# Reordering the casts, splits and sums of one expert's second layer in a kernel whose order is written out by hand

## The chip, the cores and the metric

The kernel runs on one core of a Trainium2 chip. The metric is the device time of one execution in microseconds (us), the median of several runs. Beside the times there is a profile of one execution, taken by the hardware profiler. Its engines are PE (TensorE matmul), PEld (TensorE weight load, which overlaps PE), DVE (VectorE), ACT (ScalarE), POOL (GpSimd) and SP (SyncE, which only issues DMAs here). Every engine takes its instructions strictly in the order in which the kernel emits them, and waits at one whose inputs are not ready, whatever stands behind it.

## The reference

```python
def reference(q, k, v, domain_probs, w1, w2):
    x = pooled_attention(q, k, v) + local_attention(q, k, v)   # [2, 8, 576, 64] each
    x = x.transpose(0, 2, 1, 3).reshape(1152, 512)
    p = domain_probs / (domain_probs.sum(-1, keepdims=True) + 1e-09)
    out = 0
    for e in range(4):                                         # four experts, every token
        h = np.maximum(x @ w1[e], 0.0)                         # 512 -> 1024
        out += p[:, e:e + 1] * (h @ w2[e])                     # 1024 -> 512
    return out                                                 # [1152, 512] float32
```

## The kernel before

The kernel computes the attention first, then the four experts, which the code numbers e = 0 to 3; the second expert is e = 1. Each layer of an expert is computed on 2x2 blocks with seven block products in place of eight, in the manner of Strassen: sums and differences of blocks of the tokens (or of H, the hidden rows) are multiplied with sums and differences of weight blocks. The products of a layer are called "1" to "7"; the second layer takes them in the order 1, 5, 2, 6, 7, 4, 3, so the first is "1" and the fourth is "6". To keep float32 accuracy each operand is split in two float32r tiles: a high part (a cast) and a low part (the operand minus its high part). A product is three passes of matmuls: low x high, high x low, high x high.

Each product of the second layer is done in two halves of 256 tokens. All work is cut into named steps, and one list, ORDER, gives the order in which steps are emitted; a step goes to the instruction queue of its engine. The steps around the change, with e = 1 as the first digit after the letters (for s, c and dt as shown):

- `s110`, `s111`, `s510`, `s511`, `s210`, `s211`, `s610`, `s611`, `s710`: on PE (L1239), 24 matmuls each: the two halves of the products 1, 5, 2, 6 and 7. `c11` and `c21` (L1252, 24 matmuls each) do the 128 tokens in the middle.
- `ah120.0`, `ah121.0`, `ah160.0`, `ah161.0`: on ACT (L1146, L1150), the high part of H for product 2 (halves 0 and 1) and product 6, 128x1024 each. They write a "unit" tile; there are three such tiles in a ring, so each cast waits for the matmuls that read the same tile three halves earlier: `ah120.0` waits for `s111`, `ah121.0` for `s510`, `ah160.0` for `s511`, `ah161.0` for `s210`.
- `ao120.0`, `ao121.0`, `ao160.0`, `ao161.0`: on DVE (L1155, L1159), the low parts of the same. `s210` needs `ao120.0`, `s211` needs `ao121.0`, `s610` needs `ao160.0`, `s611` needs `ao161.0`.
- `as16.0`, `as16.1`, `as17.0`: on DVE (L1133), the sums of H blocks for the products 6 and 7. `ah160.0` needs both `as16` steps.
- `bl12.0`, `bl13.0` (SP, L1093) and `bl17.1` (POOL, L1095, an adding DMA): load the raw second-layer weights of products 2, 3 and 7 into one raw buffer, so `bl13.0` waits for `bo12` and `bl17.1` for `bo13`.
- `bh12`, `bh13`, `bh17` (ACT, a cast at L186) and `bo12`, `bo13`, `bo17` (DVE, L1101): the high and low parts of these weights. `s210` needs `bo12`; `s710` needs `bo17`; `bo13` is needed only after `s710`.
- `dt1x10`, `dt1x11`, `dt1y0` (ACT, L1297, two instructions each): copy a finished PSUM bank, scaled, into a part tile; `dd1x10`, `dd1x11` (POOL, L1300) add the part tile to the accumulator by DMA. There is one part tile, so `dt1x11` waits until `dd1x10` has landed, and `dt1y0` until `dd1x11` has. `s610` needs `dt1x10`, `s611` needs `dt1x11`.
- `th1` (ACT, L1210) and `to1` (DVE, L1212): the middle tokens' high and low parts, which `c11` needs; `tdh1` (ACT, L1218) and `tdo1` (DVE, L1220) the same for `c21`.

The rules that tie a cast to its ring tile and to its inputs, in the code's own words:

```python
                    deps = deps + users[RING[n % 3]]
                    step(f"ah{e}{m}{h}.{g}", "A", deps, lambda m=m, h=h, fs=fs: high(m, h, fs))
                    step(f"ao{e}{m}{h}.{g}", "V", [f"ah{e}{m}{h}.{g}"], lambda m=m, h=h, fs=fs: low(m, h, fs))
                users[RING[n % 3]] = [f"s{m}{e}{h}"]
```

and the loop that emits the program:

```python
    for name in order(steps):
        steps[name][2]()
```

Of the kernel before, what the change touches and what calls it, by code (L numbers as in the profile page):

```python
# [68 lines left out]
    p612 wo13 p512 t1212 h2111 wm204 p712 wl20 t2212 as15.0 p113 p212 t1113 bh15 p613 h1112 wa2042 bo15 p513 t1213  # L69
    dd0y1 ao110.0 h2212 p713 t2213 p312 h2213 ah110.1 p412 h1212 ao110.1 ah111.1 ao111.0 ao111.1 s110 ah150.0 h2112  # L70
    p413 bl12.0 h2113 ao150.0 bh16 bo16 p213 wm206 p313 wm205 wa2052 bl14.1 h1113 as15.1 h1213 ah150.1 s111 ah151.0
    wa2023 ao150.1 ah151.1 ao151.0 dt1x10 ao151.1 th1 as16.0 dd1x10 bh12 bo12 bl13.0 s510 ah120.0 as16.1 bh13 ao120.0
    s511 ah121.0 bo13 ao121.0 bl17.1 s210 ah160.0 wa2020 ao160.0 dt1x11 as17.0 s211 ah161.0 dd1x11 ao161.0 s610
    ah170.0 to1 ao170.0 tr1 s611 ts1 ah171.0 d1x20.0 wa2062 d1x20.1 bh17 ao171.0 c11 dt1y0 bo17 bh14 dd1y0 d1x21.0
    bl21.0 ah140.0 d1x21.1 as13.0 s710 tdh1 tdo1 ao140.0 s711 ah141.0 d1x30.1 wh20 d1x30.0 ao141.0 c21 ah130.0 bo14
    dt1y1 d1x31.1 bl26.0 d1x31.0 dd1y1 wo20 s410 ao130.0 wl21 s411 d1z10.0 ah131.0 d1z10.1 d1z11.0 d1z11.1 ao131.0
# [1338 lines left out]
```

## Time and profile before

| what | value |
|---|---|
| time, median of 3 runs | 441.28 us (441.1 to 443.62) |
| profiled execution, its own time | 439.78 us |
| span of the profiled execution | 438.1 us |
| PE busy | 430.1 us (98% of the span) |
| DVE busy | 337.7 us (77%) |
| ACT busy | 224.2 us (51%) |
| POOL busy | 107.8 us (25%) |
| DMA | 46.72 MB, mean 107 GB/s |

The span runs from the first to the last recorded instruction; the profiled execution's own time is 1.68 us longer than its span. Busy shares are averages over stages with different limits, so they only say which engine to look at first; what a change in one place is worth has to be read from the instructions in that place.

### The profile page before, as it was taken

How to read it: one execution, taken by the hardware profiler on the slowest of the kernel's cores; microseconds unless marked ns; L12 is line 12 of the kernel's file. 1: busy time of each engine (PE TensorE's matmuls, PEld its weight loads, DVE VectorE, ACT ScalarE, POOL GpSimd, SP SyncE). 2: the span in 40 equal slices, each digit the busy share in tenths (PEclk: the TensorE clock that was granted, in tenths of full speed). 3: DMA queues.
4: the chain of work that ended last, by engine and by line, in shares of the span. 5: the costliest groups of instructions: out<-in, count | busy, mean ns of one | idle time of the engine just before them, and what ended most of it. 6: DMA issues, size and time to landing. Idle time of an engine off the chain costs nothing.

```text
span 438.1 us, 10188 instructions
## 1 busy us (share of the span) xinstructions
PE 430.1 (98%) x4221; PEld 412.7 (94%) x4221; DVE 337.7 (77%) x560; ACT 224.2 (51%) x430; POOL 107.8 (25%) x133
## 2 busy tenths in 40 slices
PE   8999999999999999999989999999999999999997
PEld 8757998998999999999989999999999999999996
DVE  2778989989899988464989874669899736688983
ACT  3547576435567634444456253555564355446540
POOL 4148781423212120021331211023312110013010
PEclk9999999999999999999999999999999999999999
DMA  9889934337708464343764854066746731145135
GB/s 170 154 242 178 171 80 94 61 87 170 143 0 121 113 146 104 49 102 79 120 97 86 177 112 74 1 156 114 104 84 137 131 76 22 49 96 79 20 97 168
DMA packets 81784, 46.72 MB, mean 107 GB/s; under 512 B 37194, under 2 KB 80714, under 8 KB 81738
## 3 DMA queue, kind: packets, MB, share of 16 engines
q1 hardware_dynamic: 63674, 29.95, 27.4%
q0 software_dynamic: 18064, 16.12, 25.8%
q8 instruction: 33, 0.54, 0.5%
q14 instruction: 13, 0.11, 0.1%
HBM read 39.63 MB, written 2.36 MB: 96 GB/s over the span
## 4 chain that ended last, share of the span: by engine, by line
PE 93%; DVE 3%; ACT 2%; DMA 1%; issue 1%; POOL 0%; ACTq 0%; POOLq 0%
PE ps L1239 34%; PE ps L1046 30%; PE ps L1252 5%; PE m02h L833 5%; PE m01h L833 4%; PE m00h L833 3%; PE wps L275 2%; PE vs L480 1%; DVE slot L1101 1%; DMA raw<-in_moe_w_dram 1%; PE a_qt L404 1%; ACT slot L186 1%; PE a_qt L402 1%; PE k01t L402 1%; PE k00t L402 1%; PE a1pv L646 1%
## 5 line engine op out<-in xcount | busy, mean ns | idle before, releaser
L1239 PE MATMUL ps<-slot,unit 128*128 128x256 f32 x1344 | 161.6, 281 | 2.4 <-DVE unit L1155 2.4
L1239 PEld LDWEIGHTS ps<-slot,unit 128*128 128x128 f32 x1344 | 160.0, 189 | 2.9 <-DVE unit L1155 2.8
L1046 PE MATMUL ps<-xhi,slot 128*128 128x288 f32 x384 | 66.5, 295 | 0.0
L1095 POOL DMA_DIRECT2D raw<-in_moe_w_dram x20 | 27.0, 1350 | 146.1 <-DVE slot L1101 112.5
L1046 PE MATMUL ps<-xc,slot 128*128 128x288 f32 x432 | 60.2, 295 | 0.0
L1046 PEld LDWEIGHTS ps<-xc,slot 128*128 128x128 f32 x432 | 58.2, 188 | 0.0
L1046 PEld LDWEIGHTS ps<-xhi,slot 128*128 128x128 f32 x384 | 56.2, 188 | 0.0
L186 ACT CAST slot<-raw 128x1024 fp32r<-128x1024 f32 (+1 forms) x40 | 49.1, 1237 | 13.0 <-DVE raw L994 4.8
L1058 ACT ACTIVATE H<-ps 128x288 f32<-128x288 f32 x72 | 27.9, 412 | 50.5 <-PE ps L1046 49.2
L1062 DVE TENSOR_TENSOR H<-H,ps 128x288 f32<-128x288 f32 x72 | 29.7, 449 | 19.6 <-PE ps L1046 19.6
L1146 ACT ACTIVATE unit<-H 128x512 fp32r<-128x512 f32 (+1 forms) x32 | 26.4, 844 | 32.2 <-DVE H L1062 18.7
L1101 DVE TENSOR_TENSOR slot<-raw,slot 128x1024 fp32r<-128x1024 f32 x28 | 34.1, 1225 | 9.9 <-ACT slot L186 9.9
L1000 DVE TENSOR_TENSOR slot<-raw,slot 128x1792 fp32r<-128x1792 f32 x12 | 24.3, 2021 | 22.2 <-PE ps L1046 18.6
L1046 PE MATMUL ps<-xlo,slot 128*128 128x288 f32 x192 | 41.1, 295 | 0.0
L1150 ACT ACTIVATE unit<-H 128x1024 fp32r<-128x1024 f32 x24 | 25.2, 1059 | 30.4 <-PE ps L1239 15.7
L1133 DVE SCALAR_TENSOR_TENSOR H<-H 128x1024 f32<-128x1024 f32 (+1 forms) x24 | 37.6, 1575 | 0.8 <-ACT H L1060 0.5
L1159 DVE SCALAR_TENSOR_TENSOR unit<-H,unit 128x1024 fp32r<-128x1024 f32 x24 | 29.3, 1220 | 7.4 <-ACT unit L1150 7.4
L988 POOL DMA_DIRECT2D raw<-in_moe_w_dram x12 | 18.4, 1594 | 52.1 <-DMA raw<-in_moe_w_dram 52.1
L1155 DVE SCALAR_TENSOR_TENSOR unit<-H,unit 128x512 fp32r<-128x512 f32 (+1 forms) x32 | 29.8, 952 | 1.4 <-ACT unit L1146 1.3
L1046 PEld LDWEIGHTS ps<-xlo,slot 128*128 128x128 f32 x192 | 30.8, 188 | 0.0
L1265 DVE SCALAR_TENSOR_TENSOR acc<-ps,npr,acc 128x256 f32<-128x256 f32 x56 | 24.3, 476 | 4.7 <-PE ps L1239 4.7
L1252 PE MATMUL ps<-slot,slot 128*128 128x256 f32 x192 | 24.3, 282 | 0.0
(290 smaller groups left out, 591.4 us busy)
## 6 DMA issues: line engine op xcount, KB each, us to landing
raw<-in_moe_w_dram POOLq DMA_DIRECT2D x20, 512.0 KB, 6.2
raw<-in_moe_w_dram SPq DMA_DIRECT2D x16, 512.0 KB, 4.0
raw<-in_moe_w_dram SPq DMA_DIRECT2D x24, 256.0 KB, 3.9
vw<-in_v_dram SPq DMA_DIRECT2D x44, 64.0 KB, 3.5
acc<-in_q_dram SPq DMA_DIRECT2D x12, 192.0 KB, 4.3
acc<-in_k_dram SPq DMA_DIRECT2D x12, 192.0 KB, 4.8
out_dram<-acc SPq DMA_DIRECT2D x18, 128.0 KB, 1.8
raw<-in_moe_w_dram SPq DMA_DIRECT2D x2, 1024.0 KB, 6.6
```

The costliest lines, as they stand in the source:

```text
L186: nc.scalar.copy(out_, in_)
L833: nc.tensor.matmul(ps[:, :n], w[:, d, cc:cc + P], x[:, d, n0:n0 + n], start=i == 0 and d == 0, stop=i == 2 and d == HP - 1,)
L1046: nc.tensor.matmul(bank(acc_, n, i)[:, :NH // 2], w[:, d * P:(d + 1) * P], x[:, d, n * (NH // 2):(n + 1) * (NH // 2)], start=u == 0 and fi ...
L1058: nc.scalar.mul(dst, at, -1.0)
L1062: nc.vector.tensor_tensor(dst, dst, at, ALU.add)
L1095: nc.gpsimd.dma_start(raw2(q), src, accum_op=ALU.add)
L1101: engine(f"bo{e}{m}").tensor_tensor(w2tile(m, 1), raw2(q), f32(w2tile(m, 0)), ALU.subtract)
L1133: nc.vector.scalar_tensor_tensor(at[o], at[x], 0.0, at[y], ALU.max, op)
L1155: nc.vector.scalar_tensor_tensor(o, x, 0.0, y, ALU.max, ALU.subtract)
L1159: nc.vector.scalar_tensor_tensor(o, x, -1.0, y, ALU.mult, ALU.subtract)
L1239: nc.tensor.matmul(ps[:, t * 256:t * 256 + 256], a[:, f, t * P:t * P + P], b[:, f], start=first_ and (t, f, x) == (0, 0, 0), stop=(t, f, x ...
L1252: nc.tensor.matmul(w, a[:, 2 * f + r], b[:, f], start=(c, r, f, x) == (1, 1, 0, 0), stop=(r, f, x) == (0, 3, 2), skip_group_check=True,)
```

## The change

Two lines of ORDER are changed, and nothing else. They cover the stretch from the last casts of product 5 to the fourth product of expert 1.

```diff
-    wa2023 ao150.1 ah151.1 ao151.0 dt1x10 ao151.1 th1 as16.0 dd1x10 bh12 bo12 bl13.0 s510 ah120.0 as16.1 bh13 ao120.0
-    s511 ah121.0 bo13 ao121.0 bl17.1 s210 ah160.0 wa2020 ao160.0 dt1x11 as17.0 s211 ah161.0 dd1x11 ao161.0 s610
+    wa2023 ao150.1 ah151.1 ao151.0 bh12 ao151.1 bo12 bl13.0 ah120.0 dt1x10 ao120.0 th1 as16.0 dd1x10 s510 ah121.0
+    as16.1 ao121.0 s511 ah160.0 ao160.0 bh13 bo13 bl17.1 s210 wa2020 dt1x11 as17.0 s211 ah161.0 dd1x11 ao161.0 s610
```

Sorted by engine, this is what changes. The orders on PE, POOL and SP stay the same.

```
ACT before: ah151.0 ah151.1 dt1x10 th1 bh12 ah120.0 bh13 ah121.0 ah160.0 dt1x11 ah161.0
ACT after:  ah151.0 ah151.1 bh12 ah120.0 dt1x10 th1 ah121.0 ah160.0 bh13 dt1x11 ah161.0
DVE before: ao151.0 ao151.1 as16.0 bo12 as16.1 ao120.0 bo13 ao121.0 ao160.0 as17.0 ao161.0
DVE after:  ao151.0 ao151.1 bo12 ao120.0 as16.0 as16.1 ao121.0 ao160.0 bo13 as17.0 ao161.0
```

## Rows read from the trace of the kernel before

**Rows 1.** Groups of instructions by line: busy us, mean ns, idle before and releaser.
```profile
L1239 PE MATMUL ps<-slot,unit 128*128 128x256 f32 x1344 | 161.6, 281 | 2.4 <-DVE unit L1155 2.4
L1239 PEld LDWEIGHTS ps<-slot,unit 128*128 128x128 f32 x1344 | 160.0, 189 | 2.9 <-DVE unit L1155 2.8
```
**Rows 2.** Timeline of PE: start, us, instructions, idle before and releaser.
```profile
209.30 8.71 PE L1239 MATMUL ps<-slot,unit 128*128 128x256 f32 x72
218.87 3.13 PE L1239 MATMUL ps<-slot,unit 128*128 128x256 f32 x24 [0.86 <-DVE unit L1155]
223.56 8.77 PE L1239 MATMUL ps<-slot,unit 128*128 128x256 f32 x72 [1.56 <-DVE unit L1155]
232.16 3.04 PE L1252 MATMUL ps<-slot,slot 128*128 128x256 f32 x24
235.04 5.86 PE L1239 MATMUL ps<-slot,unit 128*128 128x256 f32 x48
240.73 3.04 PE L1252 MATMUL ps<-slot,slot 128*128 128x256 f32 x24
```
**Rows 3.** Chain of work that ended last, from 200 us: start, us, what.
```profile
216.57 3.47 DMA raw<-in_moe_w_dram
...
221.14 1.23 DVE slot L1101
222.37 1.15 DVE unit L1155
```
**Rows 4.** Timeline of DVE.
```profile
211.65 1.90 DVE L1157 TENSOR_TENSOR unit<-H,unit 128x512 fp32r<-128x512 f32 x3
...
215.31 1.23 DVE L1101 TENSOR_TENSOR slot<-raw,slot 128x1024 fp32r<-128x1024 f32 x1 [0.63 <-ACT slot L186]
216.46 1.22 DVE L1133 SCALAR_TENSOR_TENSOR H<-H 128x1024 f32<-128x1024 f32 x1
217.59 1.22 DVE L1155 SCALAR_TENSOR_TENSOR unit<-H,unit 128x1024 fp32r<-128x1024 f32 x1
...
224.56 2.28 DVE L1133 SCALAR_TENSOR_TENSOR H<-H 128x2048 f32<-128x2048 f32 x1
...
232.69 1.22 DVE L1101 TENSOR_TENSOR slot<-raw,slot 128x1024 fp32r<-128x1024 f32 x1
...
236.81 0.68 DVE L1220 TENSOR_TENSOR slot<-H,slot 128x512 fp32r<-128x512 f32 x1
```
**Rows 5.** Timeline of ACT.
```profile
212.56 0.84 ACT L1297 ACTIVATE part1x<-ps,pr 128x256 f32<-128x256 f32 x2
213.28 1.06 ACT L1210 ACTIVATE slot<-H 128x1024 fp32r<-128x1024 f32 x1
214.24 1.05 ACT L186 CAST slot<-raw 128x1024 fp32r<-128x1024 f32 x1
215.17 1.07 ACT L1146 ACTIVATE unit<-H 128x1024 fp32r<-128x1024 f32 x1
220.06 1.05 ACT L186 CAST slot<-raw 128x1024 fp32r<-128x1024 f32 x1 [3.83 <-DMA raw<-in_moe_w_dram]
...
231.57 0.83 ACT L1297 ACTIVATE part1y<-ps,pr 128x256 f32<-128x256 f32 x2
```
**Rows 6.** Timeline of POOL.
```profile
213.69 1.20 POOL L1300 DMA_DIRECT2D acc<-part1x  x1 [1.95 <-ACT part1x L1297]
222.67 1.28 POOL L1095 DMA_DIRECT2D raw<-in_moe_w_dram  x1 [7.78 <-DVE slot L1101]
...
224.13 2.30 POOL L1300 DMA_DIRECT2D acc<-part1x  x1
```
**Rows 7.** SP's weight loads at L1093, 190 to 245 us: instructions, then time to landing.
```profile
L1093 SPq DMA_DIRECT2D raw<-in_moe_w_dram x4: 368/368/368, 195.6 to 241.8; - x4
...
DMA to landing us min/median/max: 3.5/4.2/4.9
```
**Rows 8.** POOL's adding weight loads at L1095, 205 to 250 us: time to landing.
```profile
DMA to landing us min/median/max: 5.8/5.8/6.9
```
**Rows 9.** POOL's adding DMAs of the part tiles at L1300, whole span: time to landing.
```profile
DMA to landing us min/median/max: 3.7/4.3/6.4
```

## The prediction

> **What bounds the kernel now.** I read the page first: PE is busy nearly all the span, so an edit that moves no matmul can only pay where PE stands still. The second view is the groups by line. The second layer's matmuls (L1239) stood still for 2.4 us in the whole execution, all of it for DVE's low parts at L1155 [rows 1]. The third view, PE's timeline, puts this idle time in one place, the second layer of expert 1: 0.86 us ahead of `s210` at 218.87 and 1.56 us ahead of `s211` at 223.56 [rows 2]. So the change works on the only stretch of the second layers where PE waits, and its ceiling is the price of these two gaps.
>
> The chain that ended last says where the second gap comes from. `bo12` lets `bl13.0` go, which lands 3.47 us later; ACT had been standing at `bh13` for 3.83 us; then `bo13`, and only behind it `ao121.0`, for which PE waits [rows 3, 5]. But `s211` doesn't need `bh13` or `bo13` at all: their weights are for product 3, the last of the seven. They are only queued ahead of what it needs. The first gap has the same form with less in front: `ao120.0` ran at 217.59 to 218.81, behind `as16.0`, `bo12` and `as16.1` [rows 4], and `s210` does not need the sums.
>
> **What the gaps are worth.** From `s211` to `c11` three halves took 232.16 - 223.56 = 8.60 us, so an undisturbed half takes 2.87 us from start to start. `s111`, `s510` and `s511` ran from 209.30 in one piece, so `s210` could start at 209.30 + 8.60 = 217.90 and `s211` at 220.77. It started at 223.56: the two gaps delay all that follows by 2.79 us [rows 2]. The two idle figures add up to 0.86 + 1.56 = 2.42 us, less, since a matmul's end overlaps the next one's start. The ends of matmuls in this trace are modelled and the starts recorded; I take 2.79 and keep 2.42 as the low end.
>
> The weight loads of the same line stood still for 2.8 us for the same releaser [rows 1]. [...]
>
> **The change, step by step.** Nothing is added or removed; I lay the same instructions in the new order, with start-to-start distances of the old one. On ACT these are 0.72 for a drain pair, 0.96 for a cast after `th1` and 0.93 between casts (I take 0.96 for each cast) [rows 5]; on DVE 1.15 after a weight split and 1.13 after a sum [rows 4].
>
> ACT is free for the first moved step at 212.56 [rows 5]. `bh12` now takes that place; `bl12.0`, the first of the four loads, left at 195.6 and even the slowest took 4.9 us [rows 7], so its data are there. `bh12` runs 212.56 to 213.61, `ah120.0` 213.52 to 214.59 (`s111`, whose tile it takes, ended about 212.2), `dt1x10` from 214.48, `th1` from 215.20, `ah121.0` 216.16 to 217.23 (`s510` ended about 215.0).
>
> DVE ends the low parts of product 5 at 213.55 and meets `bh12`'s end at 213.61 [rows 4], so the new wait in front of `bo12` costs it under 0.1 us. Then `bo12` 213.63 to 214.86, `ao120.0` 214.78 to 216.00, `as16.0` from 215.91, `as16.1` 217.04 to 218.26, `ao121.0` 218.17 to 219.39. PE wants `ao120.0` at 217.90 and `ao121.0` at 220.77: spare time 1.9 and 1.4 us, where both were late. **Both gaps close: -2.79 us.**
>
> What is late next? I follow each queue past the end of the change.
>
> `ah160.0` needs `as16.1` (218.26) and `s511` (about 218.0): 218.3 to 219.36; `ao160.0` ends about 220.6, wanted by `s610` at 223.63. Spare 3.0.
>
> `bh13` is now queued behind it. `bl13.0` leaves when `bo12` ends, about 214.9 in place of 216.57, and lands 3.5 to 4.9 us later, 218.4 to 219.8 [rows 3, 7]; ACT gets there at 219.3. So the 3.83 us stall of ACT becomes at most 0.5. `bo13` 220.5 to 221.7 (at most 222.1), then `as17.0` from 221.66, 2.90 us earlier than its 224.56 [rows 4], and `ao161.0` 223.9 to 225.1, wanted by `s611` at 226.50. Spare 1.4 (1.0 with the slow landing). DVE was full behind `as17.0` and moves by as much as PE does.
>
> `dt1x10` and so `dd1x10` come later: in the old order the DMA left at 213.69, 0.29 after the drain's end [rows 5, 6]; now at 215.6. With 3.7 to 6.4 us to landing [rows 9] it lands at 219.3 to 222.0, and `dt1x11` stands for it on ACT, which gets there at 220.2. This is a **new wait of 0 to 1.8 us**, with `ah161.0` queued behind. `ah161.0` then ends by 223.8, and DVE wants it at 223.9: covered, barely in the slow case, and PE only at 226.50.
>
> `bl17.1` follows `bo13` and so moves by only 0.6 us. It leaves 0.3 us after it, at 222.0, and lands 5.8 to 6.9 us later [rows 3, 6, 8]: 227.8 to 228.9. `bh17` needs 1.05 more, 230.0 at the latest; `bo17`, at 232.69 before [rows 4], has its turn at 232.69 - 2.90 = 229.8 and ends by 231.3. `s710` wants it at 235.04 - 2.79 = 232.25. Spare 0.95 to 1.2; it was 1.1.
>
> `dd1x11` stands 1.46 us behind `bl17.1` on POOL [rows 6], so it leaves at 223.5 and with the longest landing, 6.4 [rows 9], is there at 229.9. `dt1y0` waits for it and would stand on ACT at 231.57 - 2.79 = 228.8 [rows 5]: a second new wait of up to 1.1 us. Behind it comes what `tdo1` and `c21` need; `tdo1` ended at 237.49, 3.2 us ahead of `c21` [rows 2, 4]. Covered.
>
> **The sum.** -2.79 us, nothing given back. The profiled execution would go from 439.78 to 437.0, its span from 438.1 to 435.3. Its time lay 1.5 below the median of the runs, 441.28, so I subtract from the median: 438.5 us, 0.6% faster. About 1% is what a measurement of this kernel can tell from no change, so the step counts as "within 1%" although I expect it to be real.
>
> **Rivals.** (a) *The gap is moved on, in part.* The tightest spare times left are about 1 us (`ao161.0`, `bo17`). For it: two ACT waits that the old order didn't have, and `bl17.1` moving less than PE. Against: all landings of the trace fit. A landing 1 us beyond the longest, or some tenths at each of five steps, would leave 0.5 to 1.5 us of the gain lost: about 439.5.
>
> (b) *Slower: ACT held at `dt1x11` by the part tile.* `dd1x10` now leaves after `bl13.0`, not 2.9 us before it. `s611` is hurt only if `ah161.0` ends after 225.2, that is if `dd1x10` lands after 223.4, 7.8 us from its issue; each further us is then 1 us on PE. It eats the whole gain at 10.6 us; at 13 us, twice the longest in the trace, the kernel is 2.4 us slower, 443.7. Against: no landing of this line is above 6.4 [rows 9]. [...]
>
> (c) *The change doesn't do what it says*: another wait, hidden behind those shown (a shared semaphore, a dependency of the sums of H on the casts that read the same tile), keeps `ao121.0` near 222. Then 441 to 441.5. The rows speak against it: `ao120.0` and `ao121.0` start within 0.1 us of the end of the DVE work ahead of them [rows 3, 4], so queueing held them, not data.
>
> **How the numbers follow.** Full recovery 0.80 (438.5; 438.9 with the low end of the price), (a) 0.11, (b) 0.04, (c) 0.05. The range: below, the full 2.79 and about 1.0 for the scatter of a median (the three runs lay between 441.1 and 443.62), 437.5; above, (a) at its far end, 440.0, with the same scatter, 441.0. Faster by over 1% would take 4.4 us, more than all the idle time in reach: 0.04 for scatter alone. Slower by over 1% needs (b) at its far end or a scattered median: 0.04. Within 1%: 0.92.
>
> **What would show it.** Right: in the changed kernel's timeline of PE seven halves (168 matmuls) from `s111` to `s611` stand in one piece, some 20.1 us long, and the groups by line show near 0 idle at L1239; ACT no longer stands at `bh13`; `bo13` runs behind `ao160.0`; PE's last matmuls come 2.8 us earlier. `dt1x11` may show a wait for a DMA. Wrong: a gap at `s611` or `s710`, whose releaser names rival (a) or (b); a gap still at `s211` means (c); no gap and the same time would mean that the idle time was given back in the experts behind.

## The result and the profile after

The changed kernel takes 436.51 us in the median of 9 runs (436.07 to 439.43), the kernel before 441.1 us beside it (439.61 to 443.62): a ratio of 0.9907, 95% interval 0.988 to 0.9935. (A ratio and its interval, here and below, come from the single runs, without any that lies over 1.5% above the fastest of its kernel; the quotient of the two medians is 0.9896.) It is faster, as forecast, but by 3 to 5 us where 2.8 was said, and 436.5 lies below the range that was given, 437.5 to 441. The profiled execution went from 439.78 to 436.1 us.

The groups by line in the changed kernel: the second layer's matmuls wait for nothing any more, where there were 2.4 us [rows 1].

```profile
L1239 PE MATMUL ps<-slot,unit 128*128 128x256 f32 x1344 | 160.9, 280 | 0.0
L1239 PEld LDWEIGHTS ps<-slot,unit 128*128 128x128 f32 x1344 | 159.8, 189 | 0.1
```

PE's timeline of the changed kernel (start, us, instructions): the seven halves from `s111` to `s611` stand in one piece.

```profile
208.54 20.09 PE L1239 MATMUL ps<-slot,unit 128*128 128x256 f32 x168
228.47 3.04 PE L1252 MATMUL ps<-slot,slot 128*128 128x256 f32 x24
231.35 5.86 PE L1239 MATMUL ps<-slot,unit 128*128 128x256 f32 x48
```

From `s111` to `c11` it takes 228.47 - 208.54 = 19.93 us, where it took 232.16 - 209.30 = 22.86 [rows 2]: 2.93 us, near the 2.79 of the forecast. The spans differ by 438.1 - 434.4 = 3.7. The other 0.76 is there before the change begins: `s111` itself starts 0.76 us earlier, after instructions that are the same in both kernels.

ACT's timeline of the changed kernel, from `bh12` on (add 0.76 to a time to compare it with the rows of before):

```profile
211.80 1.05 ACT L186 CAST slot<-raw 128x1024 fp32r<-128x1024 f32 x1
212.75 1.05 ACT L1146 ACTIVATE unit<-H 128x1024 fp32r<-128x1024 f32 x1
213.72 0.82 ACT L1297 ACTIVATE part1x<-ps,pr 128x256 f32<-128x256 f32 x2
...
215.38 1.05 ACT L1146 ACTIVATE unit<-H 128x1024 fp32r<-128x1024 f32 x1
217.63 1.06 ACT L1150 ACTIVATE unit<-H 128x1024 fp32r<-128x1024 f32 x1 [1.20 <-DVE H L1133]
218.59 1.03 ACT L186 CAST slot<-raw 128x1024 fp32r<-128x1024 f32 x1
219.53 0.83 ACT L1297 ACTIVATE part1x<-ps,pr 128x256 f32<-128x256 f32 x2
...
229.42 0.84 ACT L1297 ACTIVATE part1y<-ps,pr 128x256 f32<-128x256 f32 x2 [1.12 <-DMA acc<-part1x]
```

And DVE's:

```profile
212.88 1.23 DVE L1101 TENSOR_TENSOR slot<-raw,slot 128x1024 fp32r<-128x1024 f32 x1
214.02 1.22 DVE L1155 SCALAR_TENSOR_TENSOR unit<-H,unit 128x1024 fp32r<-128x1024 f32 x1
215.16 2.35 DVE L1133 SCALAR_TENSOR_TENSOR H<-H 128x1024 f32<-128x1024 f32 x2
217.43 1.22 DVE L1155 SCALAR_TENSOR_TENSOR unit<-H,unit 128x1024 fp32r<-128x1024 f32 x1
218.72 1.23 DVE L1159 SCALAR_TENSOR_TENSOR unit<-H,unit 128x1024 fp32r<-128x1024 f32 x1
219.86 1.22 DVE L1101 TENSOR_TENSOR slot<-raw,slot 128x1024 fp32r<-128x1024 f32 x1
...
229.12 1.22 DVE L1101 TENSOR_TENSOR slot<-raw,slot 128x1024 fp32r<-128x1024 f32 x1
```

`ao120.0` ends at 215.24 and `ao121.0` at 218.65; PE comes to `s210` at 208.54 + 8.6 = 217.1 and to `s211` at 220.0, so both are early by 1.9 and 1.4 us, as worked out. `bh13` (218.59) no longer stands for its load. `dt1x11` (219.53) shows no wait for `dd1x10`, and `dt1y0` (229.42) shows the second new wait, 1.12 us, hidden. Everything behind `c11` only moves: from its start to the end of the span it takes 438.1 - 232.16 = 205.9 us before and 434.4 - 228.47 = 205.9 after.

So the mechanism was there and the gain in one profile had the right size. What was open was the difference between the times, over 4 us against 2.9.

### The profile page after: what moved, and what is told of

The parts are those of the page before. It is cut to its first block, busy times and chain, and to the rows that moved or that the text cites. A ratio compares the mean times of both kernels' runs of the same rounds, so it can differ in the third digit from the quotient of the medians.

```text
span 434.4 us, 10187 instructions
## 1 busy us (share of the span) xinstructions
PE 429.2 (99%) x4221; PEld 412.2 (95%) x4221; DVE 337.8 (78%) x560; ACT 224.2 (52%) x430; POOL 107.8 (25%) x133
## 4 chain that ended last, share of the span: by engine, by line
PE 97%; DVE 1%; ACT 1%; issue 0%; POOL 0%; POOLq 0%; ACTq 0%
PE ps L1239 36%; PE ps L1046 31%; PE ps L1252 5%; PE m02h L833 5%; PE m01h L833 4%; PE m00h L833 3%; PE wps L275 2%; PE vs L480 1%; PE a_qt L404 1%; PE a_qt L402 1%; PE k01t L402 1%; PE k00t L402 1%; PE a1pv L646 1%; PE a3pv L646 1%; PE a3sl L562 0%; PE a2sl L562 0%
## 5 line engine op out<-in xcount | busy, mean ns | idle before, releaser
L1095 POOL DMA_DIRECT2D raw<-in_moe_w_dram x20 | 27.0, 1351 | 142.8 <-DVE slot L1101 108.1
```

Source lines behind the costliest of these rows:

```text
L1095: nc.gpsimd.dma_start(raw2(q), src, accum_op=ALU.add)
```

## The experiments

The theory at the start: the change is worth the gap, 2.9 us, and the rest is chance ahead of it. Its first rival: the new order itself shortens what stands ahead of it. The first four runs also take the two halves of the change apart. Kernels that were timed together share the runs of the kernel before.

**e1 and e2: both kernels again, unchanged.**

> The kernel before, unchanged, timed once more as a kernel of its own. It measures what two identical kernels differ by, and gives a second profile of the stretch before the change. Theory P (the change is worth 2.9 us, read from s111's start to c11's start: 22.86 us before, 19.93 us after; the rest of the 4.6 us between the medians is scatter of the stretch before the change, which is the same code in both): no difference from before within 0.3%, s111 to c11 at 22.8 to 22.9 us again, and the start of s111 anywhere within about 1 us of 209.3. Rival S (the new order makes the stretch ahead of it shorter too, by 0.76 us in the profile): s111 starts near 209.3 again in every kernel that has the old order, and near 208.5 in every one that has the new.

> The changed kernel, unchanged, timed once more beside the kernel before. Theory P: s111 to c11 at 19.9 us again; start of s111 scattered as in the kernel before; ratio near 0.9934 (2.9 us of 441). Rival S: start of s111 near 208.5, ratio near 0.9907 again (4.1 us).

e1: ratio 1.0012 (0.9988 to 1.0036), as it must be. e2: 436.89 us, 0.9907 (0.9873 to 0.994), as in the first series. 2.9 us, a ratio of 0.9934, lies at the edge of either interval, so one series alone would not have refuted the theory; the same 4 us twice speak against it. PE's timeline in the profile of e1, and the load in its chain of waits:

```profile
209.67 8.70 PE L1239 MATMUL ps<-slot,unit 128*128 128x256 f32 x72
219.24 3.12 PE L1239 MATMUL ps<-slot,unit 128*128 128x256 f32 x24 [0.86 <-DVE unit L1155]
224.45 8.77 PE L1239 MATMUL ps<-slot,unit 128*128 128x256 f32 x72 [2.10 <-DVE unit L1155]
```
```profile
216.94 4.00 DMA raw<-in_moe_w_dram
```

In the same kernel the second gap is 2.10 us this time, not 1.56, because `bl13.0` landed after 4.00 us and not after 3.47 [rows 3]; the first gap, which waits for no DMA, is 0.86 again. In e2 `s111` to `c11` took 19.93 us again, and `s111` began at 209.21, 0.67 later than in the first profile of the same kernel: what stands ahead of the change scatters by itself. So each side missed one of its signs: the theory the ratio, the rival the early start of `s111`.

**e3: the first half of the change alone.**

```diff
-ACT: dt1x10 th1 bh12 ah120.0 bh13 ah121.0 ah160.0    DVE: as16.0 bo12 as16.1 ao120.0 bo13 ao121.0 ao160.0
+ACT: bh12 ah120.0 dt1x10 th1 bh13 ah121.0 ah160.0    DVE: bo12 ao120.0 as16.0 as16.1 bo13 ao121.0 ao160.0
```

> Only the weights and operand of product 2's first half go forward (bh12, ah120.0 ahead of dt1x10 and th1; bo12, ao120.0 ahead of as16.0); bh13 and bo13 stay ahead of ah121.0 and ao121.0. Theory P: the gap ahead of s210 closes (0.97 us). bl13.0 leaves 1.7 us earlier too, so bh13 begins at about 218.4 to 219.8 on the time axis of before, bo13 ends at 220.7 to 222.1 and ao121.0 at 221.8 to 223.2, for which s211 waits from 220.8: a gap of 1.0 to 2.4 us is left, 0.4 to 1.9 us gained, s111 to c11 21.0 to 22.4 us. If the waits were not those of the queue (rival: a hidden dependency of ao121.0), the second gap would keep its end at 223.56 and the gain would be 0.

**e4: the second half alone.**

```diff
-ACT: dt1x10 th1 bh12 ah120.0 bh13 ah121.0 ah160.0    DVE: as16.0 bo12 as16.1 ao120.0 bo13 ao121.0 ao160.0
+ACT: dt1x10 th1 bh12 ah120.0 ah121.0 ah160.0 bh13    DVE: as16.0 bo12 as16.1 ao120.0 ao121.0 ao160.0 bo13
```

> Only bh13 and bo13 go back, behind ah160.0 and ao160.0; the start of the stretch keeps the old order (dt1x10, th1, bh12, ah120.0; as16.0, bo12, as16.1, ao120.0). Theory P: s210 waits as before, until 218.87 (0.97 us lost), and s211 no longer, since ao121.0 ends at about 220.0 and s211 is due at 221.7: 1.8 to 1.9 us gained, s111 to c11 about 21.0 us. If the second gap were set by something other than the order of bo13 and ao121.0, 0 to 0.5 us gained.

PE's timeline in e3, then in e4:

```profile
211.85 11.58 PE L1239 MATMUL ps<-slot,unit 128*128 128x256 f32 x96
224.98 8.77 PE L1239 MATMUL ps<-slot,unit 128*128 128x256 f32 x72 [1.55 <-DVE unit L1155]
233.58 1.60 PE L1252 MATMUL ps<-slot,slot 128*128 128x256 f32 x12
```
```profile
208.65 8.71 PE L1239 MATMUL ps<-slot,unit 128*128 128x256 f32 x72
218.22 11.65 PE L1239 MATMUL ps<-slot,unit 128*128 128x256 f32 x96 [0.86 <-DVE unit L1155]
229.70 3.04 PE L1252 MATMUL ps<-slot,slot 128*128 128x256 f32 x24
```

`s111` to `c11`: 21.73 us in e3 (its load took 4.01 us) and 21.05 in e4, both as expected; each half closes its own gap. The times: e3 440.02 us, ratio 0.9976 (0.995 to 1.0002, so its 1.1 us are not clear of no change); e4 438.09 us, 0.9934 (0.9909 to 0.9959), 2.9 us faster than before where 1.8 to 1.9 were expected. By the traces e3 should lie 21.73 - 19.93 = 1.8 us above the changed kernel (436.89 in e2, timed beside it) and lies 3.1 above. The kernels whose PE waits for `bl13.0`'s landing are slower than their profiles say; e4, whose PE does not, isn't (1.1 by the trace, 1.2 measured).

**e5: the old order, with the load early.** To let the load go early, `bh12` and `bo12` move forward with it, which takes `bo12` out of the first gap; `bh13` and `bo13` stay where they were. This separates the landing from the queues.

```diff
-... bl12.0 h2113 ao150.0 bh16 bo16 p213 wm206 p313 wm205 wa2052 ... dd1x10 bh12 bo12 bl13.0 s510 ah120.0 as16.1 bh13
+... bl12.0 bh12 h2113 ao150.0 bo12 bh16 bo16 p213 wm206 p313 wm205 bl13.0 wa2052 ... dd1x10 s510 ah120.0 as16.1 bh13
```

> The old order, with bh12, bo12 and with them bl13.0 taken some 10 us forward, into stretches where ACT and DVE stand still; bh13 and bo13 stay ahead of ah121.0 and ao121.0, and dt1x10 and th1 ahead of ah120.0. Theory L (the old order's loss is the landing time of bl13.0 on the path of ao121.0: it differs between executions, 3.47 us in the first profile of before and 4.00 in the second, and the 2.79 us of the prediction was worked out from the shortest one): with the load landed long before, no gap is left, s111 to c11 is 19.9 us, and the time is that of the changed kernel, ratio about 0.99. Rival Q (it is the place of bo13 and bh13 in the queues that costs, load or not: 2.3 us of work ahead of ao121.0): the second gap stays at 1 us or more. Rival S (the rest of the 4 us belongs to the new order): ratio 0.993 or above.

PE's and DVE's timelines in e5 (`bo13` at 216.34, `ao121.0` at 217.47, still in the old order):

```profile
208.77 20.09 PE L1239 MATMUL ps<-slot,unit 128*128 128x256 f32 x168
228.69 3.04 PE L1252 MATMUL ps<-slot,slot 128*128 128x256 f32 x24
```
```profile
216.34 1.21 DVE L1101 TENSOR_TENSOR slot<-raw,slot 128x1024 fp32r<-128x1024 f32 x1
217.47 1.22 DVE L1155 SCALAR_TENSOR_TENSOR unit<-H,unit 128x1024 fp32r<-128x1024 f32 x1
```

No gap, 19.92 us, and 436.57 us, ratio 0.9914 (0.9884 to 0.9943): the whole gain, with `bo13` still ahead of `ao121.0`. Rival Q falls: the two steps in front cost nothing once their data are there. Rival S asked for 0.993 or above, which the interval alone doesn't exclude; but the time is that of the changed kernel (436.51 and 436.89), so the old order gets all of the 4 us when its PE doesn't stand. The traces leave no other place for it: in all 17 profiles of this document the span has 205.8 to 206.0 us behind the start of `c11`, so the profiled executions differ only in the start of `s111` and in `s111` to `c11`. So all of it, seen or not in the profile, hangs on the standing of PE.

**e6 and e7: `bl13.0`'s load twice, in the old and in the new order.**

```diff
-                nc.sync.dma_start(raw2(q), src)
+                [nc.sync.dma_start(raw2(q), src) for _ in range(1 + ((e, q, block) == (1, 0, (K2, 1))))]
```

> The old order, with bl13.0's load issued twice, one after the other into the same buffer, so that the data are there a second landing later. Theory L: each us of landing is a us of PE, so the second gap grows by a landing, 3.5 to 4.9 us: s111 to c11 at 26.3 to 28.3 us, time 3.5 to 5 us above before. Against L: less than 2 us more.

> The changed order, with the same second load. The prediction gave the landing of bl13.0 some 2.3 us of spare time in the new order (0.9 until ACT comes to bh13, 1.4 until s611 wants ao161.0). Theory L: with two landings of 3.5 to 4.9 us each, the data are there at 221.9 to 224.7 on the axis of before in place of 218.4 to 219.8; a gap of 1.1 to 3.8 us appears ahead of s611, none ahead of s210, s211 or s610; s111 to c11 21.0 to 23.7 us, so less than half of what the old order loses. If the spare times were wrong: 4 us or more lost, or nothing.

e7's timeline of PE, and its two loads in the chain of waits:

```profile
208.62 17.27 PE L1239 MATMUL ps<-slot,unit 128*128 128x256 f32 x144
227.61 3.08 PE L1239 MATMUL ps<-slot,unit 128*128 128x256 f32 x24 [1.72 <-DVE unit L1159]
230.53 3.04 PE L1252 MATMUL ps<-slot,slot 128*128 128x256 f32 x24
```
```profile
214.22 4.30 DMA raw<-in_moe_w_dram
...
218.53 3.36 DMA raw<-in_moe_w_dram
```

e7: 21.91 us, a gap ahead of `s611` and nowhere else. The data came 7.67 us after the first issue; with 2.3 us of spare time behind the expected 3.5 the point of decision is 5.8, so 1.9 us were due and 21.91 - 19.93 = 1.98 came. 438.16 us, ratio 0.9935 (0.9905 to 0.9965). e6: 444.48 us, ratio 1.009 (1.0058 to 1.0122), 4.3 us above before, in the range expected; but its `s111` to `c11` took 28.0 us, and the landings, 7.15 us from the first issue to the second landing, account only for 22.86 + 7.15 - 3.47 = 26.5. The missing 1.5 us are in the 72 matmuls behind the gap, 10.22 us long where they took 8.77 [rows 2]: in this profile the granted clock (the third figure from the end of these rows) is 0.56 and 0.59 in the 4 us from 227 on, and 1.00 in the stretches on both sides.

```profile
227.32 10.22 PE L1239 MATMUL ps<-slot,unit 128*128 128x256 f32 x72 [5.25 <-DVE unit L1155]
```
```profile
227.00:229.00 2.00, 1.68 (x8) 1.68 (x9) 2.00 (x3) 1.45 (x3) 2.00 (x3) 0.56 0.27 27
229.00:231.00 2.00, 2.00 (x12) 2.00 (x12) 2.00 (x2) 0.00 (x0) 1.19 (x1) 0.59 1.20 189
```

That pointed to the clock. The list of all executions has each one's mean clock. Of the kernel before, 25 of 68 executions in the series up to e12 had 0.995 or 0.996, with a mean time of 442.0 us; 41 had 0.999 or 1.0 and 440.1 us; two had 0.992 and took 445.4 and 446.2 us. Of the changed kernel's 15 runs (9 with the result, 6 in e2) and e5's 6 none was at 0.996 or below, nor of e4's 12 or e7's 8; of e3's 12, four were. All profiles of before so far happened to be executions with 0.999 or 1.0.

**e8 to e11 and e13 to e15: single profiles**, for the landing and in search of such an execution.

> The kernel before once more, for one more profile. Theory L: s111 to c11 is 22.86 us plus the landing time of bl13.0 less 3.47 us, to within 0.1 us, whatever the landing is; the start of s111 scatters by itself.

> The kernel before once more, for the landing time of bl13.0 and the start of s111 in another execution. Theory L: s111 to c11 is 22.86 us plus (landing less 3.47 us), within 0.1 us, as in the three profiles so far (landing 3.23, 3.47, 4.00 us: 22.61, 22.86, 23.39 us); and over all profiles the landing lies above 3.47 us more often than below. Rival C (chance ahead of the change): the landing stays near 3.5 us and the start of s111 takes up the rest, 209.2 to 210.5 in executions of this order against 208.5 to 209.2 in those of the new one, though the instructions ahead of it are the same.

> As e9: the kernel before, for the landing time of bl13.0 and the start of s111. Theory L: s111 to c11 is 22.86 us plus (landing less 3.47 us), within 0.1 us. Rival C: the start of s111 carries the difference, the landing stays near 3.5 us.

> The changed kernel once more. Theory L: s111 to c11 at 19.9 us whatever the landing of bl13.0 is; the start of s111 in the same range as in the kernel before, 208.5 to 210. Rival C: the start of s111 below 209.2 again.

> The kernel before, for a profile of an execution with the lower mean clock (0.995 or 0.996; a third of its executions so far). Theory G: in such a profile the granted clock is below 1 only in the stretch right behind s211's start, and s211 to c11 takes 10.0 to 10.4 us in place of 8.6. In a profile with a clock of 1.0: 8.6 us, and s111 to c11 at 22.86 us plus (landing less 3.47 us).

> As e13: if the mean clock is 0.995 or 0.996, s211 to c11 takes 10.0 to 10.4 us; if it is 1.0, 8.6 us.

> As e13: if the mean clock is 0.995 or 0.996, s211 to c11 takes 10.0 to 10.4 us; if it is 1.0, 8.6 us.

| profile of the kernel before | bl13.0 to landing, us | s111 to c11, us | start of s111, us | mean clock |
|---|---|---|---|---|
| e8 | 3.23 | 22.61 | 209.15 | 0.999 |
| e13 | 3.35 | 22.74 | 208.65 | 1.0 |
| first | 3.47 | 22.86 | 209.30 | 1.0 |
| e10 | 3.49 | 22.88 | 209.52 | 1.0 |
| e15 | 3.49 | 22.88 | 210.15 | 0.999 |
| e9 | 3.89 | 23.29 | 208.93 | 1.0 |
| e1 | 4.00 | 23.39 | 209.67 | 1.0 |
| e14 | 4.30 | 25.18 | 209.52 | 0.996 |

Where the clock stays up, the stretch is 19.39 us plus the landing, to 0.01 us. e11, the changed kernel:

```profile
210.10 20.09 PE L1239 MATMUL ps<-slot,unit 128*128 128x256 f32 x168
```

19.93 us again, and `s111` starts as late as in the kernel before: its eight profiles have a mean start of 209.4, the three of the changed kernel 209.3. So rival C, by which the start carries the difference, falls.

e14 is the execution that was looked for. Its timeline of PE, its load, and its busy times by stretch (length, then PE, PEld, DVE, ACT, POOL, granted clock, DMA share, GB/s):

```profile
219.09 3.14 PE L1239 MATMUL ps<-slot,unit 128*128 128x256 f32 x24 [0.86 <-DVE unit L1155]
224.61 10.26 PE L1239 MATMUL ps<-slot,unit 128*128 128x256 f32 x72 [2.38 <-DVE unit L1155]
234.70 3.04 PE L1252 MATMUL ps<-slot,slot 128*128 128x256 f32 x24
```
```profile
216.79 4.30 DMA raw<-in_moe_w_dram
```
```profile
222.00:224.00 2.00, 0.23 (x2) 0.02 (x1) 1.81 (x2) 2.00 (x4) 0.28 (x1) 1.00 0.01 4
224.00:226.00 2.00, 1.39 (x9) 1.40 (x10) 2.00 (x3) 1.73 (x4) 2.00 (x3) 0.84 0.09 10
226.00:228.00 2.00, 2.00 (x11) 2.00 (x10) 2.00 (x2) 0.00 (x0) 1.47 (x2) 0.50 1.12 166
228.00:230.00 2.00, 2.00 (x16) 2.00 (x15) 2.00 (x2) 0.68 (x1) 0.00 (x0) 0.81 1.32 191
230.00:232.00 2.00, 2.00 (x19) 2.00 (x18) 1.75 (x3) 0.90 (x2) 0.89 (x1) 1.00 0.59 92
```

PE stood for 0.86 us, worked 3.1, stood for 2.38, and just behind that the granted clock fell to 0.50. Between 226 and 228 it began 11 matmuls, between 230 and 232 it was 19. The 72 matmuls took 10.26 us in place of 8.77: 1.49 us lost after the gap itself was over; `s211` to `c11` took 10.09 us, as expected for such an execution. In the stretches that cover the execution from 0 to 430 us the granted clock is 1.00 in all but the three from 224 to 230 (0.84, 0.50 and 0.81; 0.83 over the 10 us from 220 to 230). And 19.39 + 4.30 + 1.49 = 25.18, the table's last row.

**e12: a gap of middle length.** A quarter of the load is issued again behind it.

```diff
-                nc.sync.dma_start(raw2(q), src)
+                [nc.sync.dma_start(raw2(q)[:, :, :w], src[:, :, :w]) for w in ((256, 64) if (e, q, block) == (1, 0, (K2, 1)) else (256,))]
```

> The old order, with a quarter of bl13.0's load issued a second time behind it: a gap between those of before (1.3 to 2.1 us ahead of s211) and of the load issued twice (5.25 us). Theory G (the granted clock falls behind the gap, the more often the longer PE stands): the second gap is 3.5 to 4.5 us, most executions, over three quarters, have a mean clock of 0.996 or less, and the median is 2.5 to 4.5 us above before: 2 to 2.4 us for the landing and the rest for the clock. Rival: the lower clock comes by chance and from elsewhere: a third of the executions, as before, and a median 2 to 2.4 us above before.

```profile
227.01 10.94 PE L1239 MATMUL ps<-slot,unit 128*128 128x256 f32 x72 [4.61 <-DVE unit L1155]
```
```profile
225.00:227.00 2.00, 0.00 (x0) 0.00 (x0) 2.00 (x3) 2.00 (x4) 0.88 (x2) 0.50 0.00 0
227.00:229.00 2.00, 1.99 (x9) 1.99 (x10) 2.00 (x2) 1.14 (x2) 2.00 (x3) 0.50 0.41 54
```

The gap came out at 4.61 us, a little longer than meant. Here the clock has fallen while PE still stands (0.50 between 225 and 227 us), and all 8 executions have a mean clock of 0.996 or 0.992, where chance from elsewhere would have given a third. 444.17 us, ratio 1.0079 (1.0053 to 1.0105), 4.2 above before, in the range expected. The lower clock follows the gap: none of the 41 timed executions of the changed kernel, e4, e5 and e7 has it, where PE stands at most once in this stretch, for 0.86 or 1.72 us in the profiles; all 14 of e6 and e12 have it.

## Why the prediction was wrong where it was

**Right:** what bounds the kernel, the two gaps and their cause, that both close, and the spare times behind them. The size of a gap in the profiled execution, 2.79 forecast, 2.93 measured, is right to 5%. The new waits behaved as priced: `dt1x11` none in the first profile and 0.15 us in e11 (0 to 1.8 was the range), `dt1y0` 1.12 us and hidden, `bl17.1` leaving at 221.38 + 0.76 = 222.1 on the old axis (222.0 forecast). e7 tested the spare times directly and found them right to 0.1 us. Rivals (a), (b) and (c) didn't come true; (b)'s arithmetic, applied to `bl13.0`, is what e7 shows. "Within 1%", with its chance of 0.92, held only just by the ratio (0.93% faster), and by the medians not (1.04%).

**Wrong:** the size of the sum's one term and the step that used it, "so I subtract from the median". It took one execution's gap, 2.79 us, off the median of many, as if the 1.5 us by which that median lay above the profiled execution had nothing to do with the gap. Some 0.9 us of it had. The term was too small in two ways:

- The landing. I priced the second gap with 3.47 us, though my own row gave 3.5 to 4.9 for that queue's loads [rows 7]; I used that spread for the cost side only. The eight profiles have a mean of 3.65. That is about 0.2 us.
- The clock behind the gap, which stood in no term. 25 of 68 executions have the lower mean clock, and the one that was caught in a profile, e14, lost 1.49 us by it behind the gap. These 25 were 442.0 - 440.1 = 1.9 us longer; that the other 0.4 us are long landings, as in e14, is not shown. Over all executions 1.9 us are 1.9 x 25/68 = 0.7 us.

How much of the gain this explains: the 41 executions with the clock up average 440.1, the 21 runs of the changed kernel and of e5 436.9, so 3.2 us for the gaps; with 0.7 for the clock 3.9, a ratio of 0.991 (measured 0.9907, 0.988 to 0.9935). That only splits the measured difference in two and proves nothing by itself. The traces give a sum of their own: the seven profiles of before with the clock up have a mean of 22.95 us from `s111` to `c11`, 3.0 more than 19.93, and 1.49 x 25/68 is 0.55, together 3.6. The remaining 0.3 to 0.5 us have no trace that shows them.

The range failed with the same step: its low end allowed 1.0 us for scatter, as if that were of both signs alike, but the scatter of the kernel before was in good part a cost of the gap, on one side only, and the change took it away. Chance had a part in how far the time missed: 441.28, the first median of before, was 0.4 above that of the longer series (440.85), which I could not know, and 436.51 is 0.4 below the 436.89 of e2. But 436.89 lies below the range too.

What stays open: only one profile of the kernel before, e14, shows the clock of such an execution, beside the 68 that were timed, and none shows one with 0.992. That the 25 lose it at the same place is inferred from their mean clock and from e4, e5 and the changed kernel, where the gap is short or gone and no execution has it.

## What to carry to other kernels

A wait in a profile that ends with a DMA is one draw (the same load landed after 3.23 to 4.30 us in eight profiles here): price it with the spread of landings on that queue, and use the spread on the gain's side as well as on the cost's. If a kernel's runs lie above their profiled execution, ask what the stall under study does in the executions that were not profiled; a mean clock lower by 0.4 to 0.5% in some of them was the sign here. A step that waits for data needed later belongs behind the steps that are needed now, or its load has to be started earlier: both gave the same time here, 436.51 and 436.57 us.

## What the runs showed of the hardware

That PE's granted clock falls after so short a standstill was not expected: in e14 it fell to 0.50 after gaps of 0.86 and 2.38 us within 7 us, while in the profiles of the kernel before with second gaps of 1.3 to 2.1 us it did not (mean clock 0.999 or 1.0); with 4.61 and 5.25 us in the profiles of e12 (0.50) and e6 (0.56 and 0.59) the mean clock was 0.996 or lower in all 14 timed executions. e7, with a single gap of 1.72 us, had none in 8, e3 (1.55 us in its profile) four in 12. Equal programs came out with and without the lower clock: of the kernel before 25 of 68 executions had a mean of 0.995 or 0.996, 41 had 0.999 or 1.0. What decides between the two is not shown. The landing of the same load at the same place took 3.23 to 4.30 us in the eight profiles of one program. The start of `s111` scattered from 208.54 to 211.85 us over the kernels whose instructions ahead of it are identical (all but e5); the cause stays open.
